# Row 0 of a dilated sliding attention in two halves of 288 tokens, with its loads and row 1's let go in a new order, ahead of a ReLU-squared MLP

## The chip, the cores and the metric

The kernel runs on one core of one Trainium2 chip. The metric is the device time of one execution in microseconds (us). A profile is taken of one execution; its span is about 1.8 us shorter than the time of that execution. TensorE is called PE below, VectorE DVE, ScalarE ACT, GpSimd POOL and SyncE SP, as in the profile.

## The reference, cut to what matters

```python
# q, k, v: (8 rows, 8 heads, 576 tokens, 64); heads 0-3 sliding, 4-7 dilated
scores = scale * np.matmul(q, k.transpose(0, 1, 3, 2))
mask_plain = (rel >= 0) & (rel < 32)
mask_dil   = (rel >= 0) & (rel < 128) & (rel % 4 == 0)
attn = softmax(where(mask, scores, -1e9));  x = attn @ v     # 4608 tokens x 512
h = x @ w_in                                                 # 512 x 2048
out = (np.maximum(h, 0.0) ** 2) @ w_out                      # 2048 x 512
```

A "row" is one of the eight batch rows, 576 tokens; a "chunk" is 512 of the 4608 tokens, one unit of the MLP. Chunk 0 needs nothing but row 0; chunk 1 needs row 1 as well. The first product is `x @ w_in`, the second is with `w_out`.

## The kernel before

The program is in fixed order on each engine. A generator of product matmuls is "pumped": each `pump(n)` puts n small pieces of product work between pieces of attention. A load that must not start too early is let go by a memset into its target on DVE: the load waits for the memset, and the memset for all DVE work in front of it.

```python
load_sliding_qk(0, (nc.sync, nc.scalar))       # row 0, whole
load_dilated_qk(0); load_sliding_v(0); load_dilated_v(0, nc.scalar)
...
transposes_and_scores(0, idle_and_load)        # w_in let go at the third call
...
load_sliding_qk(1); load_dilated_qk(1)         # row 1, right behind row 0
g0 = hidden(0)
pending.append(mm1_part_gen(0, g0, 0, 288))    # chunk 0's first product, tokens 0-287
for a in range(2):
    pump(1); zs.append(av_dilated(0, 1, a))    # row 0's second half beside it
pump(1); x_sliding(0, 1, xs, False)
pump(2); x_dilated(0, 1, zs, False); pump(8)
...; load_w_out(); pump(1000)
pending.append(mm1_part_gen(0, g0, 288, TOKC)) # tokens 288-511
pump(2)
reload_v(1)                                    # row 1's v let go here
pump(1); cast_sliding_qk(1, ...); pump(2)
transposes_and_scores(1, lambda: pump(1)); pump(1000)
pending.append(mm2_by_rows_gen(0, g0)); pump(3)
scores_dilated(1, lambda: pump(3))
...; dk = keep_qk(2)                           # row 2's q, k to scratch
pump(12); cast_v(nc.scalar); attn_values(1, rows_and_load, True)
```

The softmax here doesn't subtract the row's maximum and nothing guards it: scores larger than these inputs give would overflow.

## Time and profile before

| What | Value | Where it is read |
|---|---|---|
| time | 307.47 us, median of 4 (307.22 to 307.62) | runs |
| PE busy | 295.0 us, 96% of the span | busy table of the page |
| row 0's keys landed | 8.26 us | chain in order of time |
| first product starts (half of row 0) | 25.73 us | chain |
| all of row 0 ready | 29.84 us | timeline of ACT |
| v of row 1 let go, landed | 36.2, 54.4 us | timeline of SP, chain |
| chunk 1's first product starts | 64.94 us | chain |

In the chain each line is a start, a length and a piece of work, followed back from the last instruction to what released it. A DMA that stands there means that the program was waiting for it. Behind 64.94 us the two kernels do the same work. The whole difference therefore lies in front of that point. I call that part the opening.

### The profile page before, as it was taken

Reading aid. Unit: us, or ns where it says so; the run is one execution under the profiler, and the core shown is the slowest. Engines: PE = TensorE matmul, PEld = TensorE weight load, DVE = VectorE, ACT = ScalarE, POOL = GpSimd, SP = SyncE. Lnnn points to the kernel's source line nnn. Section 1 sums busy time; section 2 is a strip of 40 time slices with the busy share of each in tenths; the row PEclk is TensorE's granted clock in tenths of the full one; section 3 lists DMA queues with packets and bytes.
Section 4 is the critical chain, followed back from the end, with each engine's and each line's share of the span. In section 5 each row is a group of like instructions: output and inputs, shape, how many; then the busy total and the mean of one; then the engine's idle time right before and its main releaser. Section 6 shows DMA issues by size and latency. Waiting matters only on the chain.

```text
span 307.1 us, 7069 instructions
## 1 busy us (share of the span) xinstructions
PE 295.0 (96%) x2920; PEld 199.0 (65%) x2920; DVE 213.7 (70%) x428; ACT 184.6 (60%) x317; POOL 41.9 (14%) x86
## 2 busy tenths in 40 slices
PE   6789999999899999999999999999999999999995
PEld 2777774444597459745974597459745974684484
DVE  5487682479976697769776977697769775834744
ACT  2586893668933894389438953895389526505610
POOL 4312302006002300230023002300100010000000
PEclk9599999999999999999999999999999999999998
DMA  7999899899979989999859993979520012003004
GB/s 183 249 210 226 142 179 211 186 224 224 276 147 240 266 143 221 226 225 155 178 168 226 152 231 113 228 173 181 142 96 2 0 40 99 2 0 140 0 0 139
DMA packets 83312, 47.91 MB, mean 156 GB/s; under 512 B 67792, under 2 KB 79568, under 8 KB 82896
## 3 DMA queue, kind: packets, MB, share of 16 engines
q1 hardware_dynamic: 75060, 26.12, 41.3%
q0 software_dynamic: 6848, 19.80, 28.3%
q10 hardware_dynamic: 1372, 1.54, 1.8%
q8 instruction: 23, 0.38, 0.5%
q14 instruction: 9, 0.07, 0.1%
HBM read 39.85 MB, written 16.52 MB: 184 GB/s over the span
## 4 chain that ended last, share of the span: by engine, by line
PE 86%; DMA 6%; ACT 3%; SPq 2%; DVE 1%; issue 1%; DVEq 0%; ACTq 0%
PE ph L324 37%; PE pob L374 9%; PE poa L374 9%; PE poe L374 5%; PE poc L374 5%; PE pod L374 5%; DMA sv<-in_v_dram 3%; PE paw L621 3%; PE ph L302 3%; DMA sq<-in_k_dram 2%; SPq L106 2%; PE pav L607 2%; PE py L654 2%; PE ps L556 1%; PE px L636 1%; PE po L345 1%
## 5 line engine op out<-in xcount | busy, mean ns | idle before, releaser
L324 PE MATMUL ph<-xT,wi 128*128 128x512 f16 x512 | 115.8, 379 | 0.0
L290 ACT ACTIVATE rt<-ph 128x512 f16<-128x512 f32 x128 | 75.5, 602 | 32.9 <-PE ph L324 32.6
L324 PEld LDWEIGHTS <-wi 128*128 128x128 f16 x512 | 48.2, 98 | 55.1
L294 DVE TENSOR_TENSOR g<-rt 128x1024 f16<-128x1024 f16 x56 | 38.7, 691 | 35.2 <-ACT rt L290 34.9
L374 PEld LDWEIGHTS <-sm 128*128 128x128 f16 x512 | 47.0, 98 | 4.9
L374 PEld LDWEIGHTS <-g 128*128 128x128 f16 x384 | 35.8, 98 | 6.5 <-DVE g L292 1.1
L374 PE MATMUL pob<-T,sm 128*128 128x256 f16 x256 | 32.5, 272 | 0.0
L374 PE MATMUL poa<-wo,g 128*128 128x256 f16 x256 | 32.1, 273 | 0.0
L660 ACT COPY xT<-py 128x576 f16<-128x576 f16 x16 | 10.2, 638 | 25.8 <-PE py L654 25.7
L394 POOL DMA_DIRECT2D out_dram<-otl x6 | 4.5, 756 | 152.2 <-DVE otl L429 152.2
L590 DVE TENSOR_TENSOR x_d<-paw,rcp_d 72x512 f16<-72x512 f32 x32 | 22.0, 686 | 1.1
L528 ACT ACTIVATE AT<-pz 128x576 f16<-128x576 f32 x32 | 19.0, 653 | 2.3 <-PE pz L575 1.8
L528 ACT ACTIVATE AT<-ps 128x576 f16<-128x576 f32 x32 | 19.2, 659 | 0.7 <-PE ps L538 0.3
L642 ACT COPY xT<-px 128x576 f16<-128x576 f16 x16 | 10.2, 640 | 14.7 <-PE px L636 14.7
L529 DVE TENSOR_TENSOR AT<-AT,maskp 128x576 f16<-128x576 f16 x32 | 14.9, 474 | 4.5 <-ACT AT L528 3.6
L302 PE MATMUL ph<-xT,wi 128*128 128x288 f16 (+1 forms) x128 | 16.6, 272 | 0.9 <-ACT xT L660 0.5
L590 DVE TENSOR_TENSOR x_p<-pav,rcp_p 96x512 f16<-96x512 f32 x24 | 16.5, 687 | 0.8
L529 DVE TENSOR_TENSOR AT<-AT,maskd 128x576 f16<-128x576 f16 x32 | 14.1, 456 | 3.4 <-ACT AT L528 2.3
L374 PE MATMUL pod<-T,g 128*128 128x256 f16 x128 | 16.2, 272 | 0.0
L374 PE MATMUL poc<-T,sm 128*128 128x256 f16 x128 | 16.2, 272 | 0.0
L374 PE MATMUL poe<-wo,sm 128*128 128x256 f16 x128 | 16.1, 273 | 0.0
L145 ACT CAST vd<-sd 128x1024 f16<-128x1024 f32 x16 | 16.1, 1070 | 0.0
(99 smaller groups left out, 369.7 us busy)
## 6 DMA issues: line engine op xcount, KB each, us to landing
sv<-in_v_dram SPq DMA_DIRECT2D x40, 128.0 KB, 4.6
sd<-in_v_dram SPq DMA_DIRECT2D x7, 512.0 KB, 5.9
dk<-in_k_dram POOLq DMA_DIRECT2D x12, 288.0 KB, 6.6
dk<-in_q_dram POOLq DMA_DIRECT2D x12, 288.0 KB, 8.2
out_dram<-otl POOLq DMA_DIRECT2D x6, 512.0 KB, 3.6
out_dram<-otu POOLq DMA_DIRECT2D x6, 512.0 KB, 3.7
wi<-in_moe_w_in_dram POOLq DMA_DIRECT2D x2, 1024.0 KB, 12.1
wo<-in_moe_w_out_dram POOLq DMA_DIRECT2D x4, 512.0 KB, 10.1
```

The costliest lines, as they stand in the source:

```text
L145: nc.scalar.copy(o, i)
L290: nc.scalar.activation(rt[:, o, :], ph[:], ACTF.Relu)
L294: nc.vector.tensor_mul(g[:, ffc - 1 : ffc + 1, :], rt, rt)
L302: nc.tensor.matmul(ph[:, 0 : t1 - t0], wi[:, dmk, ffc * P : ffc * P + P], xs[:, dmk, :], start=(dmk == 0), stop=(dmk == NDM - 1),)
L324: nc.tensor.matmul(ph, wi[:, dmk, ffc * P : ffc * P + P], xs[:, dmk, :], start=(dmk == 0), stop=(dmk == NDM - 1),)
L374: nc.tensor.matmul(acc, lhs[:, k, t * P : (t + 1) * P], rhs[:, k, :], start=(first and k == 0), stop=(k == NK - 1), skip_group_check=True,)
L528: nc.scalar.activation(AT[:, u, 0:UW], ps[:, :, 0 : UW // 2], ACTF.Exp, scale=scale)
L529: nc.vector.tensor_mul(AT[:, u, 0:UW], AT[:, u, 0:UW], mask)
L590: nc.vector.tensor_tensor(out=x[0:w], in0=pv[:, :, :, 0:D], in1=rcp[0:w].unsqueeze(3).to_broadcast([w, 2, HH, D]), op=ALU.mult,)
L621: nc.tensor.matmul(pav[:, e, h * (D + 2) : h * (D + 2) + D + 1], AT[:, 4 + h, off : off + P], vd[:, t, 2 * a + e, h, 0 : D + 1], start=Tru ...
L642: nc.scalar.copy(xT[:, 0:2, t0 : t0 + 288], px[:, 0:UW].rearrange("x (c t) -> x c t", c=2),)
L660: nc.scalar.copy(xT[:, 2:4, t0 : t0 + 288].rearrange("x c (i r) -> x c i r", r=DIL), py[:, 0:UW].rearrange("x (c r i) -> x c i r", c=2, r= ...
```

## The change

Its intent: start row 0's attention as soon as half of its data is there, spread the loads so that each comes when it is needed, give the queues to w_in and w_out in pieces, and run chunk 0's first product in one part with row 1's transposes under it. The core of the diff, cut:

```diff
-    load_sliding_qk(0, (nc.sync, nc.scalar))
+    load_sliding_qk_half(0, 0, nc.sync)
+    load_sliding_qk_half(1, 0, nc.scalar)
...
-        for f0, f1 in ((0, 1024), (1024, 2048)):
+        for f0, f1 in ((0, 512), (512, 1024), (1024, 1536), (1536, 2048)):
...
+    cast_sliding_qk_half(1, 0, nc.scalar)
+    cast_sliding_qk_half(0, 0, nc.vector)
+    nc.vector.memset(sv[:, :, :, 0:1], 0.0)
+    nc.vector.memset(sd[:, :, :, 0:1], 0.0)
+    load_sliding_v(0, 0, 3)
+    load_dilated_v(0, nc.sync, (0,))
+    load_sliding_qk_half(1, 1, nc.sync)        # second half of q, k behind v's first
+    load_sliding_qk_half(0, 1, nc.sync)
+    load_sliding_v(0, 3, 6)
+    load_dilated_v(0, nc.sync, (1,))
... (halves of row 0, interleaved, with idle matmuls between)
+    load_w_out(0, 1)
+    load_dilated_qk(1)
+    load_w_out(1, 4)
...
     g0 = hidden(0)
-    pending.append(mm1_part_gen(0, g0, 0, 288))
...
+    pending.append(mm1_gen(0, g0))             # undivided
+    pump(10)
+    nc.vector.memset(sq[:, :, :, 0:1], 0.0)
+    load_sliding_qk(1)                         # row 1's q, k let go here
+    pump(14)
+    cast_sliding_qk(1, (nc.scalar, nc.vector, nc.scalar, nc.vector))
+    pump(2)
...
-    reload_v(1)
...
     scores_dilated(1, lambda: pump(3))
+    reload_v(1)                                # row 1's v let go here
...
-    pump(12)
+    pump(2)
     cast_v(nc.scalar)
```

More of the change, by code (lines that the diff above doesn't have):

```diff
@@ L73 @@
     wo = wpool.tile([P, NFF, DM], FP16, name="wo")
-    QKTp = const.tile([P, 2, 2, PADP + S], FP16, name="QKTp")
+    QKTp = [const.tile([P, 2, PADP + S], FP16, name=f"QKTp{hp}") for hp in range(2)]
     QKTd = const.tile([P, 2, 2, KPAD + S], FP16, name="QKTd")
@@ L86 @@
     sq = gp.tile([QB, 2, HH, 6 * D], FP32, name="sq", tag="sm")
-    early = tp.tile([QB, 2, 2, 12 * D * 2], FP16, name="early", tag="T")
-    nq_ = early[:, 0].rearrange("p i (j h d) -> p i j h d", j=6, h=HH)
-    nd_ = early[:, 1].rearrange("p i (g x) -> p i g x", g=2)
+    early = tp.tile([QB, 7168], FP16, name="early", tag="T")
+    nq_ = early[:, 0:3072].rearrange("p (i j h d) -> p i j h d", i=2, j=6, h=HH)
+    nd_ = early[:, 3072:6144].rearrange("p (i g x) -> p i g x", i=2, g=2)
+    nqh = early[:, 0:3072].rearrange("p (f i j h d) -> p f i j h d", f=2, i=2, j=3, h=HH)
+    ndh = early[0:72, 3072:7168].rearrange("p (f i g x) -> p f i g x", f=2, i=2, g=2)
     ident = const.tile([P, P], FP16, name="ident")
@@ L100, in load_sliding_qk, with load_sliding_qk_half, load_dilated_qk_half, load_sliding_v @@
             )
-    def load_sliding_v(b):
-        for m in range(NB):
+    def load_sliding_qk_half(i, f, eng):
+        eng.dma_start(
+            out=sq[:, i, :, 192 * f : 192 * (f + 1)],
+            in_=(q, k)[i][0, 0:HH, 288 * f : 288 * (f + 1), :].rearrange(
+                "h (p j) d -> p h (j d)", j=3
+            ),
+        )
+    def load_dilated_qk_half(f):
+        for i, src in ((1, k), (0, q)):
+            s4 = src[0, HH:H, 288 * f : 288 * (f + 1), :].rearrange(
+                "(g e) (p j) d -> e p g (j d)", e=2, j=8
+            )
+            for e in range(2):
+                nc.gpsimd.dma_start(out=ndh[36 * e : 36 * (e + 1), f, i, :, :], in_=s4[e])
+    def load_sliding_v(b, m0=0, m1=NB):
+        for m in range(m0, m1):
             lo = QB * m - PADP
@@ L109, in load_sliding_v, with load_dilated_v @@
             )
-    def load_dilated_v(b, eng):
+    def load_dilated_v(b, eng, ts=(0, 1)):
         vv = v[b, HH:H].rearrange("h (i c) d -> i h (c d)", c=DIL)
-        eng.dma_start(out=sd[PADD:P, 0, :, :], in_=vv[0:QD])
-        eng.dma_start(out=sd[:, 1, :, :], in_=vv[QD - PADD : CL])
+        if 0 in ts:
+            eng.dma_start(out=sd[PADD:P, 0, :, :], in_=vv[0:QD])
+        if 1 in ts:
+            eng.dma_start(out=sd[:, 1, :, :], in_=vv[QD - PADD : CL])
     def load_v(b):
@@ L131, in load_w_in, with load_w_out @@
             )
-    def load_w_out():
-        for j in range(4):
+    def load_w_out(j0, j1):
+        for j in range(j0, j1):
             nc.gpsimd.dma_start(
@@ L157, in cast_sliding_qk, with cast_sliding_qk_half @@
                 )
+    def cast_sliding_qk_half(i, f, eng):
+        copy(
+            eng,
+            nqh[:, f, i],
+            sq[:, i, :, 192 * f : 192 * (f + 1)].rearrange("p h (j d) -> p j h d", d=D),
+        )
     def cast_sliding_v(eng, step, m0=0, m1=NB):
@@ L161, in cast_sliding_v, with cast_dilated_v @@
             copy(eng, vp[:, m : m + step, :, 0:D], sv[:, m : m + step, :, :])
-    def cast_dilated_v(eng, step):
-        for t in range(2):
+    def cast_dilated_v(eng, step, ts=(0, 1)):
+        for t in ts:
             for c in range(0, DIL, step):
@@ L211 @@
     nc.scalar.activation(warm, warm, ACTF.Exp)
-    load_dilated_qk(0)
+    load_dilated_qk_half(0)
     make_identity(nc, ident)
-    load_sliding_v(0)
-    load_dilated_v(0, nc.scalar)
     relf = const.tile([P, QB], FP32, name="relf")
@@ L231 @@
         )
-    nc.vector.memset(QKTp[:, 1, :, 0:PADP], 0.0)
+    for hp in range(2):
+        nc.vector.memset(QKTp[hp][:, 1, 0:PADP], 0.0)
     nc.vector.memset(QKTx[:, 1, 0:PADP], 0.0)
-    nc.vector.memset(QKTd[:, 1, :, 0:KPAD], 0.0)
+    nc.vector.memset(QKTd[:, 1, :, :], 0.0)
     nc.vector.memset(AT[:, :, UW:640], 0.0)
@@ L505, in t_sliding @@
             nc.vector if i else nc.scalar,
-            QKTp[:, i, hp, PADP:].rearrange("x (p j) -> x p j", j=6),
+            QKTp[hp][:, i, PADP:].rearrange("x (p j) -> x p j", j=6),
             p_[:, 0:UW].rearrange("x (j p) -> x p j", j=6),
@@ L525, in t_dilated, with t_sliding_half, t_dilated_half @@
             )
+    def t_sliding_half(hp, f, eng):
+        p_ = pt(f"ph{hp}_{f}", False)
+        for i in (1, 0):
+            for j in range(3):
+                nc.tensor.transpose(
+                    p_[:, 288 * i + QB * j : 288 * i + QB * (j + 1)],
+                    nqh[:, f, i, j, 2 * hp : 2 * hp + 2, :],
+                    ident[0:QB, 0:QB],
+                )
+        t0 = PADP + 288 * f
+        copy(
+            eng,
+            QKTp[hp][:, :, t0 : t0 + 288].rearrange("x i (p j) -> x i p j", j=3),
+            p_[:, 0:UW].rearrange("x (i j p) -> x i p j", i=2, j=3),
+        )
+    def t_dilated_half(i, f, eng):
+        p_ = pt(f"pg{i}_{f}", False)
+        for g in range(2):
+            for n in range(4):
+                o = 288 * (n % 2) + 144 * (n // 2) + 72 * g
+                nc.tensor.transpose(
+                    p_[:, o : o + 72],
+                    ndh[:, f, i, g, P * n : P * (n + 1)],
+                    ident[0:72, 0:72],
+                )
+        for a in range(2):
+            copy(
+                eng,
+                QKTd[:, i, a, KPAD:]
+                .rearrange("x (g n) -> x g n", n=CL)[:, :, QD * f : QD * (f + 1)]
+                .rearrange("x g (p s) -> x g p s", s=2),
+                p_[:, 288 * a : 288 * (a + 1)].rearrange("x (s g p) -> x g p s", s=2, g=HH),
+            )
     def softmax(u, ps, mask):
@@ L529, in softmax, with s_sliding @@
         nc.vector.tensor_mul(AT[:, u, 0:UW], AT[:, u, 0:UW], mask)
-    def s_sliding(b, hp):
-        tiles = [pa(f"ps{b}_{hp}_{half}") for half in range(2)]
-        for half, ps in enumerate(tiles):
+    def s_sliding(b, hp, halves=(0, 1)):
+        tiles = [pa(f"ps{b}_{hp}_{half}") for half in halves]
+        for half, ps in zip(halves, tiles):
             for m3 in range(3):
@@ L539, in s_sliding @@
                         ps[:, e, QB * m3 : QB * (m3 + 1)],
-                        QKTp[r, 1, hp, QB * m : QB * m + P],
-                        QKTp[r, 0, hp, PADP + QB * m : PADP + QB * (m + 1)],
+                        QKTp[hp][r, 1, QB * m : QB * m + P],
+                        QKTp[hp][r, 0, PADP + QB * m : PADP + QB * (m + 1)],
                         start=True,
@@ L544, in s_sliding @@
                     )
-        for half, ps in enumerate(tiles):
+        for half, ps in zip(halves, tiles):
             softmax(2 * hp + half, ps, maskp)
@@ L583, in s_dilated, with s_dilated_half, normalize, av_sliding @@
             softmax(4 + 2 * g + h, ps, maskd)
-    def normalize(b, what, pav, w):
+    def s_dilated_half(t, g):
+        ps = pa(f"pz_{t}_{g}")
+        for h in range(2):
+            for a in range(2):
+                q0 = KPAD + (2 * g + h) * CL + QD * t
+                for e in range(2):
+                    r = slice(D * e, D * (e + 1))
+                    n = 2 * h + a
+                    nc.tensor.matmul(
+                        ps[:, e, QD * n : QD * (n + 1)],
+                        QKTd[r, 1, a, q0 - PADD : q0 - PADD + P],
+                        QKTd[r, 0, a, q0 : q0 + QD],
+                        start=True,
+                        stop=True,
+                    )
+        softmax(4 + 2 * t + g, ps, maskd)
+    def normalize(b, what, pav, w, n=2):
         x = xp.tile([QB, 2, HH, D], FP16, name=f"x{b}_{what}", tag="x")
         rcp = xp.tile([QB, 2, HH], FP32, name=f"rcp{b}_{what}", tag="rcp")
-        pv = pav[0:w, :, 0 : HH * (D + 2)].rearrange("p i (h d) -> p i h d", d=D + 2)
-        nc.vector.reciprocal(rcp[0:w], pv[:, :, :, D])
+        pv = pav[0:w, 0:n, 0 : HH * (D + 2)].rearrange("p i (h d) -> p i h d", d=D + 2)
+        nc.vector.reciprocal(rcp[0:w, 0:n], pv[:, :, :, D])
         nc.vector.tensor_tensor(
-            out=x[0:w],
+            out=x[0:w, 0:n],
             in0=pv[:, :, :, 0:D],
-            in1=rcp[0:w].unsqueeze(3).to_broadcast([w, 2, HH, D]),
+            in1=rcp[0:w, 0:n].unsqueeze(3).to_broadcast([w, n, HH, D]),
             op=ALU.mult,
         )
-        return x
-    def av_sliding(b, mp):
-        pav = pa(f"pav{b}_{mp}")
-        for i in range(2):
-            m = 2 * mp + i
+        return [x[:, i] for i in range(n)]
+    def av_sliding(b, m0, m1):
+        pav = pa(f"pav{b}_{m0}")
+        for i, m in enumerate(range(m0, m1)):
             for h in range(HH):
@@ L613, in av_sliding @@
                 )
-        return normalize(b, f"p{mp}", pav, QB)
+        return normalize(b, f"p{m0}", pav, QB, m1 - m0)
     def av_dilated(b, t, a):
@@ L619, in av_dilated @@
             for h in range(HH):
-                off = e * 288 + a * 144 + t * QD
+                if b == 0:
+                    u, off = 4 + 2 * t + h // 2, e * 288 + (h % 2) * 144 + a * QD
+                else:
+                    u, off = 4 + h, e * 288 + a * 144 + t * QD
                 nc.tensor.matmul(
                     pav[:, e, h * (D + 2) : h * (D + 2) + D + 1],
-                    AT[:, 4 + h, off : off + P],
+                    AT[:, u, off : off + P],
                     vd[:, t, 2 * a + e, h, 0 : D + 1],
@@ L633, in x_sliding @@
             m = 3 * half + m3
-            x = xs[m // 2][:, m % 2].rearrange("p h d -> p (h d)")
+            x = xs[m].rearrange("p h d -> p (h d)")
             for c in range(2):
@@ L650, in x_dilated @@
             for e in range(2):
-                x = xs[a][:, e].rearrange("p h d -> p (h d)")
+                x = xs[2 * a + e].rearrange("p h d -> p (h d)")
                 for c in range(2):
@@ L684, in attn_values @@
         for mp in range(3):
-            xs.append(av_sliding(b, mp))
+            xs += av_sliding(b, 2 * mp, 2 * mp + 2)
             fill()
@@ L688, in attn_values @@
         fill()
-        ys = [av_dilated(b, 0, 0)]
+        ys = av_dilated(b, 0, 0)
         fill()
@@ L692, in attn_values @@
         fill()
-        ys.append(av_dilated(b, 0, 1))
+        ys += av_dilated(b, 0, 1)
         fill()
@@ L696, in attn_values @@
         for a in range(2):
-            zs.append(av_dilated(b, 1, a))
+            zs += av_dilated(b, 1, a)
             fill()
@@ L704 @@
     hold = const.tile([P, 1], FP32, name="hold")
-    cast_sliding_qk(0, (nc.scalar, nc.scalar, nc.vector, nc.gpsimd))
     pj = pmool.tile([P, TOKC], FP32, name="pj", tag="pm")
-    idle_matmuls(pj, 14, TOKC)
-    def idle():
-        idle_matmuls(pj, 5, P)
-    def idle_and_load():
-        idle()
-        n_idle[0] += 1
-        if n_idle[0] == 3:
-            nc.vector.memset(hold, 0.0)
-            nc.gpsimd.memset(hold, 0.0)
-            load_w_in()
-            cast_sliding_v(nc.gpsimd, 2)
@@ L722 @@
-    n_idle = [0]
-    transposes_and_scores(0, idle_and_load)
-    scores_dilated(0, idle)
-    cast_dilated_v(nc.scalar, DIL)
-    xs = [av_sliding(0, 0)]
-    idle()
-    xs.append(av_sliding(0, 1))
-    nc.vector.memset(sq[:, :, :, 0:1], 0.0)
-    nc.vector.memset(nd_[:, :, :, 0:1], 0.0)
-    idle()
-    ys = [av_dilated(0, 0, 0)]
-    idle()
-    x_sliding(0, 0, xs, False)
-    idle()
-    ys.append(av_dilated(0, 0, 1))
-    idle()
-    xs.append(av_sliding(0, 2))
-    idle()
-    x_dilated(0, 0, ys, False)
@@ L742, with idle @@
-    load_sliding_qk(1)
-    load_dilated_qk(1)
-    g0 = hidden(0)
-    pending.append(mm1_part_gen(0, g0, 0, 288))
-    zs = []
-    for a in range(2):
-        pump(1)
-        zs.append(av_dilated(0, 1, a))
-    pump(1)
-    x_sliding(0, 1, xs, False)
-    pump(2)
-    x_dilated(0, 1, zs, False)
-    pump(8)
+    idle_matmuls(pj, 12, TOKC)
+    def idle(n=3):
+        idle_matmuls(pj, n, P)
+    cast_sliding_qk_half(1, 0, nc.scalar)
+    cast_sliding_qk_half(0, 0, nc.vector)
+    nc.vector.memset(sv[:, :, :, 0:1], 0.0)
@@ L757 @@
+    nc.vector.memset(sd[:, :, :, 0:1], 0.0)
[5 more added lines that the diff above has]
+    load_dilated_v(0, nc.sync, (1,))
+    t_sliding_half(0, 0, nc.scalar)
+    t_sliding_half(1, 0, nc.vector)
     nc.vector.memset(hold, 0.0)
     nc.gpsimd.memset(hold, 0.0)
-    load_w_out()
+    load_dilated_qk_half(1)
+    t_dilated_half(1, 0, nc.scalar)
+    idle()
+    s_sliding(0, 0, (0,))
@@ new lines @@
+    t_dilated_half(0, 0, nc.vector)
+    s_sliding(0, 1, (0,))
+    cast_sliding_v(nc.gpsimd, 3, 0, 3)
+    cast_dilated_v(nc.gpsimd, DIL, (0,))
+    load_w_in()
+    idle(4)
+    s_dilated_half(0, 0)
+    s_dilated_half(0, 1)
+    cast_sliding_qk_half(1, 1, nc.scalar)
+    cast_sliding_qk_half(0, 1, nc.scalar)
+    idle(9)
+    xs = av_sliding(0, 0, 2)
+    xs += av_sliding(0, 2, 3)
+    idle(4)
+    ys = av_dilated(0, 0, 0)
+    idle(2)
+    t_sliding_half(0, 1, nc.scalar)
+    t_sliding_half(1, 1, nc.scalar)
@@ new lines @@
+    x_sliding(0, 0, xs, False)
+    ys += av_dilated(0, 0, 1)
+    s_sliding(0, 0, (1,))
+    t_dilated_half(1, 1, nc.scalar)
+    s_sliding(0, 1, (1,))
+    t_dilated_half(0, 1, nc.vector)
+    x_dilated(0, 0, ys, False)
+    idle()
+    s_dilated_half(1, 0)
+    s_dilated_half(1, 1)
+    cast_sliding_v(nc.gpsimd, 3, 3, 6)
+    cast_dilated_v(nc.gpsimd, DIL, (1,))
+    load_w_out(0, 1)
+    load_dilated_qk(1)
+    load_w_out(1, 4)
+    idle(6)
+    xs += av_sliding(0, 3, 5)
+    xs += av_sliding(0, 5, 6)
@@ new lines @@
+    idle(4)
+    zs = av_dilated(0, 1, 0)
+    idle(4)
+    zs += av_dilated(0, 1, 1)
+    idle(4)
+    x_sliding(0, 1, xs, False)
+    idle(4)
+    x_dilated(0, 1, zs, False)
+    idle(4)
+    g0 = hidden(0)
+    pending.append(mm1_gen(0, g0))
[5 more added lines that the diff above has]
+    pump(2)
+    for hp in range(2):
+        for i in (1, 0):
+            t_sliding(1, hp, i)
+            pump(1)
@@ L760 @@
     pump(1000)
-    pending.append(mm1_part_gen(0, g0, 288, TOKC))
-    pump(2)
     def reload_v(b):
@@ L768, in reload_v @@
         load_v(b)
+    pending.append(mm2_by_rows_gen(0, g0))
+    for g in range(2):
+        s_sliding(1, g)
+        pump(2)
+        for i in (1, 0):
+            t_dilated(1, g, i, True)
+            pump(2)
+    scores_dilated(1, lambda: pump(3))
     reload_v(1)
-    pump(1)
-    cast_sliding_qk(1, (nc.scalar, nc.vector, nc.scalar, nc.vector))
+    nc.gpsimd.tensor_copy(hold, wo[:, NFF - 1, DM - 1 :])
+    nc.gpsimd.tensor_copy(hold, sd[:, 1, HH - 1, DIL * D - 1 :])
+    dk = keep_qk(2)
     pump(2)
-    transposes_and_scores(1, lambda: pump(1))
-    pump(1000)
-    pending.append(mm2_by_rows_gen(0, g0))
-    pump(3)
-    scores_dilated(1, lambda: pump(3))
-    nc.vector.memset(hold, 0.0)
-    nc.gpsimd.memset(hold, 0.0)
-    dk = keep_qk(2)
-    pump(12)
     cast_v(nc.scalar)
@@ L812 @@
                 pump(2)
+            pump(2)
         else:
```

## The prediction

> **What bounds the kernel now.** I read the page's slices first, then its chain by share, then the chain in order of time, because the change touches only the first rows. The busy tenths say that TensorE (PE) is full from the fourth slice (23 us) to the end:
>
> ```profile
> PE   6789999999899999999999999999999999999995
> PEclk9599999999999999999999999999999999999998
> DMA  7999899899979989999859993979520012003004
> ```
>
> So the time is the start-up, plus the PE work, plus PE's gaps. The change can gain only before the point at which chunk 1's first product starts, because everything behind that is the same work. In the chain in order of time (start, length, what) that point is 64.94:
>
> ```profile
> 0.75 7.51 DMA sq<-in_k_dram
> 8.28 0.96 DVE early L147
> 9.29 0.66 PE pt L499 x6
> ...
> 25.04 0.65 ACT xT L660
> 25.73 0.40 PE ph L302 x2
> ...
> 29.13 6.17 PE ph L302 x52
> ...
> 44.00 10.41 DMA sv<-in_v_dram
> 54.56 1.48 ACT vp L145
> 56.08 0.41 PE pav L607 x8
> ...
> 64.94 7.36 PE ph L324 x34
> ```
>
> Three things stand there. Row 0's queries and keys arrive at 8.3 us. The first product starts at 25.7, on half of row 0. And row 1's values land at 54.4, just as PE runs out of other work: the timeline by engine shows how small the gap is, and when the values were asked for.
>
> ```profile
> 36.18 10.99 SPq L106 DMA_DIRECT2D sv<-in_v_dram  x6
> ...
> 48.61 0.43 PE L575 MATMUL pz<-QKTd 64*128 64x72 f16 x16
> ...
> 50.59 0.06 DVE L779 MEMSET hold<- 128x1 f32 x1
> ...
> 56.08 0.41 PE L607 MATMUL pav<-vp,AT 128*128 128x65 f16 x8 [0.45 <-ACT vp L145]
> ```
>
> The loads began at 36.2, took 18 us beside w_out, and cost PE 0.45 us. From 28.1 to 64.8 the table by stretches gives DMA shares of 0.84 to 1.27 except in 33.6 to 36.2 (0.42): the queues are nearly always busy here, so when a load is let go decides what it competes with.
>
> **What the Trainium skill says.** "DMA: Bandwidth & Descriptors", section "Queues, rings and completion order": each DMA engine goes round-robin between the queues that have work for it, a packet at a time. The trace agrees: row 1's q and k, 0.59 MB each, were issued at 22.94 and 23.37 beside w_in and landed 6.9 and 11.3 us later. Same page, "Issuing engines are not separate DMA queues": moving loads between issuing engines gives no bandwidth, so taking row 0's dilated values from ACT to SP gains nothing by itself. "TensorE: Matmul & The Clock Gate", section "Architectural detail", says that ACT and DVE are strict FIFO: a memset that lets a load go waits for all earlier DVE work. The same page's "What's actually happening" gives half clock after an idle window of about 3.4 us; here PE idled 2.94 us before 9.29 (somewhat less than that window), and the table by stretches shows a clock of 0.50 from 10 to 15 us.
>
> **The change part by part.**
>
> *Undivided first product.* 52 matmuls of 288 columns took 6.17 us (119 ns each) and 8 of 224 took 0.85 to the next start (106 ns): 64 x 119 + 64 x 106 = 14.4 us. 34 of 512 columns took 7.36 us (216 ns): 64 x 216 = 13.8 us. Saved: 0.6 us of PE. But the product cannot start until both halves of row 0 are transposed.
>
> *Row 0 in halves, start T0 of the first product.* First-half q, k are 0.59 MB sliding plus 0.29 MB dilated. Summing the page's GB/s slices (1.875 us each) gives 0.37 MB by 3.75 us and 0.91 by 5.6, so they land near 5.5 instead of 8.3. But DVE's set-up, which ended at 5.4, grows by about 0.5 us (memset of all 1280 columns of the dilated keys; 512 columns took 0.27), so its cast ends near 6.95 and the transposes start at 7, 2.3 us earlier. That cast also lets the v loads go, so the queues run nearly empty for about 2 us (issue to first bytes took that long at the start: 7 GB/s in the first slice). Then v's first half (0.65 MB), dilated half 1 (0.29) and sliding half 1 (0.59) follow: 1.5 MB at 250 GB/s from 8.5 gives 14.7 us for the second q. From there its chain is: cast 0.83, transposes 0.5, two evictions on ACT 1.3, scores 0.3, four exps 2.4 interleaved with evictions 0.7 and 0.8, last mask 0.5, four normalizations 3.2 on DVE (0.9 each, the narrow one 0.5), transposes 0.4, xT copies 1.3: about 12.5 us, so 27.2. The second v half (0.92 MB, mostly 256-byte rows) starts near 15 together with w_in (2.1 MB): 3.0 MB at 210 GB/s end at 29.5, the last dilated values perhaps at 25 to 27, then 1.2 us of GpSimd cast (0.61 per 512 columns), two AV groups and a copy, 3 us: 29 to 31. I take T0 = 28 (before: all of row 0 was ready at 29.85, but 27 of the divided matmuls were done by then).
>
> *PE work behind T0.* Before, 29.85 to 64.8 is 35.0 us. Taking out 1.3 of gaps, 11.2 of first product (37 x 0.119 + 64 x 0.106) and 13.8 of second leaves 8.6 for row 1. After: T0 + 13.8 + 13.8 + 8.6 = T0 + 36.2, without gaps. At T0 = 28 that would be 64.2: a gain of 0.6 us.
>
> *Gap for row 1's q, k.* They are let go after 10 pumps (20 matmuls), and 16 pumps = 32 matmuls = 6.9 us later PE needs their casts. DVE reaches the memset some 0.6 us late, so PE gives them 6.3 us. Alone they need about 7 us as at the start (7.51), beside w_out 11.7 as in the trace; plus a cast of 0.95. Gap 1.6 to 6.3; I take 3.
>
> *Gap for row 1's v.* This is the largest term. The load moves from 36 us, early in row 1's work, to behind the last dilated scores. Those stand at T0 + 13.8 + 1.1 (transposes) + 15 pumps of second product 6.5 + score and transpose groups 1.9 = T0 + 23.3, plus the gap above. From them the trace takes 1.98 us to the next DVE memset (48.61 to 50.59); the six sliding issues of row 2 took 3.25 us with a landing of 3.2 to 4.6 us for each, so the last lands about 6.9 after the first issue; the cast takes 1.48. Sum 10.4 us. PE has 0.4 + 5 pumps = 2.5 us of work meanwhile, then waits 7.9 us. Before, it waited 0.45.
>
> *Tail.* From the first AV to chunk 1: 56.08 to 64.8, 8.7 us, unchanged. End of the stage = 28 + 23.3 + 3 + 10.4 + 8.7 = 73.4 against 64.8: +8.6 us. Row 2's scratch copy is held until v has landed, so it comes near 71 and its transposes follow some 13 us later; the two extra pumps there (0.86 us) just cover it. Sum: 307.5 + 8.6 = 316.
>
> **The rivals.** (a) *Row 0 comes in so early that it pays.* Break-even needs T0 plus the q, k gap near 22.4. For: the chain starts 2.3 us earlier, and halves overlap DMA with work. Against: from 15 to 25 us ACT (4.13 and 3.17 of each 5) and DVE (4.13 and 4.63) were already mostly busy, and that work isn't removed; DVE alone has some 14 us of it after 6. With T0 = 24 and a gap of 1.6 the sum is 3.2 us over break-even: 310.7; only a smaller v gap as well makes it 305 or less. (b) *The queues decide, not the issue order*: w_out is out of the way when v is asked for, so v lands quickly, and before it landed at 54.4 anyhow. This is true of the queue, but v is asked for at about 56 in my sum, so it costs time still; it makes 312 if T0 is 26 and the first gap 1. (c) *Clock.* PE waiting 7.9 us falls to half clock and up to 2 us of the tail are added, and v's second half comes late behind w_in (T0 = 31): 320 or more.
>
> **Range and chances.** The v gap follows from program order and I hold it nearly certain; T0 (24 to 31) and the q, k gap (1.6 to 6.3) are estimates worth several us each way. A kernel tuned this finely, with counts of idle matmuls fitted, speaks for a result not much worse, so I shade 316 to 315, with 304.5 to 321. Over 2% slower (313.7) needs T0 plus gap above 28.6: 0.56. Within 2%: 0.36. Faster by 2% needs T0 near 16 and no gap for q and k, or a slip in my reading: 0.08.
>
> **What would show it.** Step by step in the profile after: sliding q, k landing near 5.5 and the first transposes at 7; the first 512-column product near 28; a PE idle of 2 to 6 us in that product before row 1's sliding transposes, ended by casts from q or k; the v issues 2 us behind the last dilated scores of row 1, and a PE idle of 7 to 8 us ended by the cast of v; chunk 1's first product near 73. It is wrong if that product starts at 65 or sooner, or if the v loads are issued before the scores are done.

## The result, and the profile after

The changed kernel took 327.07 us (median of 4, 325.92 to 327.50) against 307.47. The ratio is 1.063, with a 95% interval of 1.060 to 1.066: slower. Ratios here are the mean time of one kernel's runs over that of the other's from the same rounds, so they are not quite the ratio of the medians quoted.

The 40 slices of the page after (8.1 us each), the same three rows as were shown of before:

```profile
PE   7589919919998999999999999999999999999995
PEclk9757987977999999999999999999999999999999
DMA  5999960087999999999896999489930003003003
```

PE has a 1 in its sixth and in its ninth slice, where before it was full from the fourth on. The clock is at 5 to 7 in several slices, and the DMA row has a 6 and two zeros in slices six to eight: the queues stand still from about 47 to 65 us, in the middle of the stretch in which they had been busy before.

The chain in order of time of the kernel after:

```profile
0.74 4.95 DMA sq<-in_k_dram
...
29.57 4.06 PE ph L352 x18
...
34.65 11.66 DMA sq<-in_k_dram
...
47.27 0.66 PE pt L527 x6
...
67.14 3.44 DMA sv<-in_v_dram
...
72.35 0.60 PE pav L687 x8
...
82.86 8.20 PE ph L352 x38
```

The first half's keys land at 5.7 us, 2.6 us sooner than the whole did. The first product nevertheless starts only at 29.57. Then the chain runs through two loads of row 1: its keys, let go at 34.65 and landed at 46.3, and its values, the last of which lands at 70.6. Chunk 1 starts at 82.86 in place of 64.94: 17.9 us later. The medians differ by 19.6 us: the profiled execution of the kernel before took 308.89 us, 1.4 us above its median, and in a later trace of the same opening (of the run with v late alone, below) what follows row 0's first transposes comes about 1.2 us sooner.

The two waits on PE's timeline, in brackets with what ended them:

```profile
47.27 0.66 PE L527 MATMUL pt<-ident,early 96*128 96x96 f16 x6 [6.75 <-ACT early L166]
...
72.35 0.60 PE L687 MATMUL pav<-vp,AT 128*128 128x65 f16 x8 [7.15 <-ACT vp L166]
```

The table by stretches of the same trace shows what PE did meanwhile (stretch; length; busy us and instruction count of PE, PE weight loads, DVE, ACT, POOL; clock; DMA share; GB/s):

```profile
40.00:47.30 7.30, 0.55 (x4) 0.06 (x3) 1.66 (x3) 1.21 (x3) 0.00 (x0) 0.89 0.86 196
47.30:53.60 6.30, 6.30 (x40) 3.44 (x42) 3.06 (x5) 3.62 (x6) 0.19 (x1) 0.58 0.01 4
53.60:65.20 11.60, 11.60 (x121) 5.81 (x121) 5.85 (x16) 6.66 (x13) 0.00 (x0) 1.00 0.01 1
65.20:72.35 7.15, 0.00 (x1) 0.00 (x0) 0.00 (x0) 1.47 (x1) 0.00 (x0) 0.81 0.88 201
72.35:82.80 10.45, 10.45 (x109) 5.86 (x109) 7.32 (x18) 6.05 (x9) 2.20 (x5) 0.80 0.65 133
```

PE is idle in the first and fourth stretch (6.75 us waiting for the casts of row 1's q and k, 7.15 us for the cast of v). In the stretch after each, the clock is 0.58 and 0.80. And from 47.3 to 65.2 the DMA share is 0.01: nothing was on the queues, and the load that PE would wait for next had not been asked for.

### The profile page after: what moved, and what is told of

Same layout as the page of the kernel before. It is cut to its first block, busy times and chain, and to the rows that moved or that the text cites. A ratio compares the mean times of both kernels' runs of the same rounds, so it can differ in the third digit from the quotient of the medians. Undisturbed runs are those within 1.5% of the kernel's fastest.

```text
span 325.1 us, 6864 instructions
## 1 busy us (share of the span) xinstructions
PE 298.6 (92%) x2823; PEld 194.7 (60%) x2823; DVE 213.2 (66%) x422; ACT 183.9 (57%) x301; POOL 48.9 (15%) x92
## 3 DMA queue, kind: packets, MB, share of 16 engines
q0 software_dynamic: 8352, 19.80, 27.2%
## 4 chain that ended last, share of the span: by engine, by line
PE 84%; DMA 8%; ACT 4%; DVE 1%; SPq 1%; issue 1%; ACTq 0%; DVEq 0%
PE ph L352 37%; PE pob L402 9%; PE poa L402 9%; DMA sq<-in_k_dram 5%; PE poe L402 4%; PE poc L402 4%; PE po L373 4%; PE pod L402 4%; PE paw L704 3%; DMA sq<-in_q_dram 2%; PE pav L687 2%; PE pz L639 2%; ACT AT L592 1%; PE px L719 1%; PE ps L620 1%; PE py L737 1%
## 5 line engine op out<-in xcount | busy, mean ns | idle before, releaser
L352 PE MATMUL ph<-xT,wi 128*128 128x512 f16 x576 | 132.4, 383 | 0.1
L318 ACT ACTIVATE rt<-ph 128x512 f16<-128x512 f32 x144 | 85.0, 601 | 36.4 <-PE ph L352 36.1
L352 PEld LDWEIGHTS <-wi 128*128 128x128 f16 x576 | 54.6, 98 | 62.0 <-issue 0.9
L322 DVE TENSOR_TENSOR g<-rt 128x1024 f16<-128x1024 f16 x63 | 43.5, 691 | 46.4 <-ACT rt L318 46.1
L687 PE MATMUL pav<-vp,AT 128*128 128x65 f16 x192 | 11.1, 206 | 8.7 <-ACT vp L166 8.3
L373 PE MATMUL po<-wo,g 128*128 128x512 f16 x64 | 18.3, 402 | 0.0
L670 DVE RECIPROCAL rcp_d<-paw 72x8 f32<-72x8 f32 x32 | 6.4, 199 | 18.0 <-PE paw L704 18.0
L671 DVE TENSOR_TENSOR x_p<-pav,rcp_p 96x512 f16<-96x512 f32 (+1 forms) x25 | 16.6, 665 | 0.9
L687 PEld LDWEIGHTS <-AT 128*128 128x128 f16 x192 | 10.2, 106 | 10.9 <-issue 10.2
```

What stands on the lines that cost most here:

```text
L318: nc.scalar.activation(rt[:, o, :], ph[:], ACTF.Relu)
L322: nc.vector.tensor_mul(g[:, ffc - 1 : ffc + 1, :], rt, rt)
L352: nc.tensor.matmul(ph, wi[:, dmk, ffc * P : ffc * P + P], xs[:, dmk, :], start=(dmk == 0), stop=(dmk == NDM - 1),)
L373: nc.tensor.matmul(po, g[:, ffc, t * P : (t + 1) * P], wo[:, ffc, :], start=(ffc == 0), stop=(ffc == NFF - 1),)
L671: nc.vector.tensor_tensor(out=x[0:w, 0:n], in0=pv[:, :, :, 0:D], in1=rcp[0:w, 0:n].unsqueeze(3).to_broadcast([w, n, HH, D]), op=ALU.mult,)
L687: nc.tensor.matmul(pav[:, i, h * (D + 2) : h * (D + 2) + D + 1], AT[:, u, off : off + P], vp[:, m, h, 0 : D + 1], start=True, stop=True,)
```

## The experiments

Theory: the time is lost because row 1's loads are let go too late and in the wrong company, which makes two waits, each with a stretch of half clock behind it. Rivals: the queues are the limit whatever the order; or row 0 in halves, or the undivided product, costs the time by itself.

### One load let go early, the other left

```diff
     load_sliding_qk(1)
+    reload_v(1)
...
-    reload_v(1)          # was behind scores_dilated(1)
```

> The changed kernel with one thing moved: row 1's value loads are let go right behind row 1's query and key loads (about 34.8 us) in place of behind row 1's last dilated scores (64.5 us). Theory (the order in which the loads are let go costs the time): the 7.15 us wait of TensorE for the cast of v goes, and with it the half clock that follows it (about 1.8 us of the 10.5 us tail, which took 8.7 before): 327 to about 318 us; the 6.75 us wait for row 1's keys stays. Rival (the queues are the limit, whatever the order): v now shares with w_out and with q and k, the wait for the keys grows by as much as the other shrinks, and the time stays at 324 us or more.

Measured: 318.86 us (317.98 to 319.39), ratio 1.036. The wait for v fell to 0.25 us and the tail (from the first value product to chunk 1) to 9.3 us; the wait for the keys stayed at 6.32 us. The rival is out: SP issued v beside the keys, from 35.65 to 48.48 us, and the keys landed no later relative to their issue (11.23 us).

```diff
     x_dilated(0, 0, ys, False)
+    nc.vector.memset(sq[:, :, :, 0:1], 0.0)
+    load_sliding_qk(1)
...
-    pump(10)
-    nc.vector.memset(sq[:, :, :, 0:1], 0.0)
-    load_sliding_qk(1)
-    pump(14)
+    pump(24)
```

> The changed kernel with row 1's query and key loads let go once row 0's second half is cast and transposed (about 22 us) in place of 10 pumps into chunk 0's first product (34.2 us); the value loads stay late. Theory: they land by about 36 us, the 6.75 us wait before row 1's transposes goes and with it about 2.6 us of half clock behind it: 327 to about 318 us. Rival (queues are the limit): the loads take bandwidth from w_in, chunk 0's first product waits for its later pieces instead, and the time stays at 324 us or more.

Measured: 319.92 us (318.90 to 320.98), ratio 1.039. The 6.75 us wait became two of 0.54 and 0.57 us. The wait for v stayed at 7.03 us. The gain of 7.2 us is 2 us short of the expectation; the two waits that are left make 1.1 of them. The first product did not wait for w_in, so the rival is out too.

### Both early: the repaired kernel

The edit is both of the above, with v let go at 10 pumps into the product.

> Both moves: row 1's queries and keys let go at about 22 us, its values 10 pumps into chunk 0's first product (about 34 us). Theory: both waits and both half-clock stretches go, 18 us in all: about 308 to 309 us, level with the kernel before, because row 0 in halves starts the product at 29.6 us with 36.2 us of work behind it against the 64.9 us of before. If row 0 in halves cost something of its own that I have not seen, 312 us or more; if it gains, 305 or less.

Measured: 310.60 us (309.82 to 311.44), ratio 1.009 (1.005 to 1.013). So 16.5 of the 19.6 us come from where two calls stand in the program. Some 3 us were left, and the expectation of "level" missed. The chain of this run shows where to look:

```profile
8.94 7.24 DMA sq<-in_q_dram
...
29.29 10.10 PE ph L352 x46
```

Row 0's second half of queries is let go at 8.94, lands at 16.18, and everything up to the product at 29.29 hangs on it.

### Why the keys took so long: w_out held back

```diff
-    load_w_out(1, 4)
...
     cast_sliding_qk(1, (nc.scalar, nc.vector, nc.scalar, nc.vector))
+    nc.gpsimd.tensor_copy(hold[0:QB, :], sq[:, 1, HH - 1, 6 * D - 1 :])
+    load_w_out(1, 4)
```

> The changed kernel with the last three quarters of w_out held until row 1's keys have landed; row 1's loads where the change has them (34.2 us). Tells why those keys take 11.7 us from issue to landing. Theory (sharing with w_out): alone they take about 7 us and land near 41.7 in place of 46.3, so the wait shrinks from 6.75 to about 2 us, too short for half clock: 327 to about 320 us. Rival (the loads are simply let go too late, and take as long alone): 325 to 327 us.

Measured: 318.94 us (318.54 to 320.20), ratio 1.037. The chain of this run has the load of the keys:

```profile
33.82 6.67 DMA sq<-in_k_dram
```

The load took 6.67 us in place of 11.66, PE waited 1.75 us, and from the first transposes to the first scores it took 3.8 us in place of 6.3. So this load was slow because it shared with w_out. That the time came out 1 us below the expectation is not the theory's merit: in this trace the first product began at 28.20 in place of 29.57. PE waited nowhere for the later w_out.

### The late v alone, in the kernel before

```diff
-    reload_v(1)          # early in row 1's work
...
     scores_dilated(1, lambda: pump(3))
+    reload_v(1)
```

> The kernel before with one part of the change alone: row 1's value loads let go behind the last dilated scores of row 1 (about 50.6 us) in place of early (36.2 us). Theory: the cast of v then ends near 61 to 62 us in place of 56.0, and TensorE, which runs out of work at 54.4 to 55.6, waits some 6 us and comes out at half clock: 307.5 to about 314 us. Rival (the queues decide when v lands, w_out is ahead of it anyway): within 1.5 us of 307.5.

Measured: 317.92 us (316.71 to 318.28), ratio 1.033: slower, as the theory said, and by 4 us more than expected. The timeline of PE in this run has the wait in brackets:

```profile
63.02 0.60 PE L607 MATMUL pav<-vp,AT 128*128 128x65 f16 x8 [8.71 <-ACT vp L145]
```

SP took 6.42 us to issue the six loads, against 3.04 in the changed kernel. In this kernel row 2's scratch copies are let go at the same point and share the queues (issued from 49.7 us, between the loads of v); the changed kernel holds them until v has landed. I had not counted that. That they are what made v slower here is argued from this order; no run separates it.

### The half clock behind the waits

The edit puts idle matmuls on zeros ahead of a wait (28 of 512 columns ahead of both, then 26 ahead of one at a time).

```diff
+    idle_matmuls(pa("fill0")[:, 0, :], 28, TOKC)   # ahead of row 1's transposes
...
+    idle_matmuls(pa("fill1")[:, 0, :], 28, TOKC)   # ahead of attn_values(1, ...)
```

> The changed kernel with 28 idle matmuls of 512 columns (6 us at full clock) put on TensorE ahead of each of the two long waits, for row 1's keys and for row 1's values; loads as in the changed kernel. The waits themselves stay, but TensorE is not idle in them. Theory: the clock granted behind them stays at full speed, worth about 2.6 us behind the first and 1.8 us behind the second: 327 to about 322.5 us. Rival (the half clock is hidden, or another engine sets the pace there): 326 to 327 us.

Measured: 326.68 us, but in two groups (324.01, 324.70, 328.65, 328.81), ratio 1.061 (1.053 to 1.069). The profiled run, of the lower group, had a clock of 1.00 in all five stretches of the table above. What made the upper group slow is open; the time decides nothing. So I filled one wait at a time.

> The changed kernel with 26 idle matmuls of 512 columns (5.6 us) ahead of the wait for row 1's keys alone. Theory: the stretch from the first transposes of row 1 to its first scores takes 3.8 us in place of 6.3, and the time falls from 327.1 to about 324.7 us. Rival (the half clock is hidden, or the work on zeros slows something else): 326.5 us or more.

Measured: 323.65 us (323.11 to 324.84), ratio 1.054. From the first transposes to the first scores it took 3.8 us in place of 6.3. That is 2.4 us; the rest of the 3.4 us is not the clock's. In this trace the keys were let go at 34.01 in place of 34.65, ahead of the edit.

> The changed kernel with 26 idle matmuls of 512 columns ahead of the wait for row 1's values alone. Theory: the tail from the first value product to chunk 1's first product takes 9.1 us in place of 10.5, and the time falls from 327.1 to about 325.7 us. Rival: 326.5 us or more.

Measured: 325.58 us (324.56 to 326.76), ratio 1.060. The tail took 9.9 us in place of 10.5, with a wait of 0.94 us for ACT in it; with both waits filled it took 9.3. The half clock is real and on the path: in the traces 2.4 us behind the first wait and 0.6 to 1.2 behind the second.

### The undivided product, in the kernel before

```diff
-    pending.append(mm1_part_gen(0, g0, 0, 288))
...
     x_dilated(0, 1, zs, False)
+    pending.append(mm1_gen(0, g0))
```

with idle matmuls in place of the pumps in front of it.

> The kernel before with one part of the change alone: chunk 0's first product undivided, starting when all of row 0 is transposed, with idle matmuls where its first part had run beside row 0's last groups. Loads keep their order. Theory: 27 of the 64 divided groups' matmuls (3.2 us) had run before all of row 0 was ready, and undividing saves 0.6 us of TensorE: 307.5 to about 310 us. Rival (undividing is free because PE has slack elsewhere): within 0.8 us of the kernel before.

Measured: 307.41 us (306.67 to 307.99), ratio 1.000 (0.998 to 1.002). My theory fell. The timeline of PE shows why:

```profile
27.19 7.93 PE L324 MATMUL ph<-xT,wi 128*128 128x512 f16 x36 [0.29 <-ACT xT L660]
```

Without the product in between, the whole of row 0 is ready at 27.1 us, not at 29.84. But not all of this is the edit's doing. The last copy of row 0 on ACT's timeline, in the kernel before, in the run with v late (whose opening is that of the kernel before) and in this run:

```profile
29.21 0.63 ACT L660 COPY xT<-py 128x576 f16<-128x576 f16 x1
27.98 0.63 ACT L660 COPY xT<-py 128x576 f16<-128x576 f16 x1
26.50 0.64 ACT L660 COPY xT<-py 128x576 f16<-128x576 f16 x1 [0.45 <-PE py L654]
```

The same opening ended 1.2 us apart in two executions; from 10 to 15 us their clock was 0.50 and 0.66. Against the second of these traces, the divided product delays row 0 by 1.5 us. That is less than the 3.2 us of its work that was done by then, and yet the times are level; the rest I did not trace. Beside this, row 0 in halves, with its product at 29.29 in the repaired kernel, is 2.1 us slower than row 0 whole. In five traces with the changed kernel's opening as it stands, all of row 0 is ready between 28.9 and 30.0 us (29.2 in the repaired kernel), so the loss is 1.8 to 2.9 us against this one trace of row 0 whole.

### What row 0 in halves lacks

Edits of the repaired kernel. First, the product divided again:

```diff
     x_dilated(0, 0, ys, False)
+    pending.append(mm1_part_gen(0, g0, 0, 288))
...
-    idle(6)
+    pump(2)
     xs += av_sliding(0, 3, 5)
... (each later idle(4) in row 0 becomes pump(1); tokens 288-511 follow as in the kernel before)
```

> The repaired kernel (both of row 1's loads early, 310.6 us) with chunk 0's first product divided again at 288 tokens, its first part put in place of the idle matmuls beside row 0's second half. Theory: row 0 in halves made all of row 0 ready no more than 0.6 us sooner, and the undivided product gave up about 3 us of product work that the kernel before had done by then; some 6 of the 16 groups of 4 (0.48 us each, 2.9 us) now run beside row 0's second half: 310.6 to about 307.5 us. Rival (ACT and DVE set the pace there, and relu and square delay row 0's chain by as much): 310 to 311 us.

Measured: 309.84 us (309.58 to 310.50), ratio 1.007. Most of the expected 3 us did not come: as I read the timelines, DVE and PE took up the product's work in row 0's chain, and 0.80 us went to a wait for w_in at 34.95.

Then, with the product undivided, the second half's q and k loaded at once:

```diff
     load_sliding_qk_half(0, 0, nc.sync)
     load_sliding_qk_half(1, 0, nc.scalar)
+    load_sliding_qk_half(0, 1, nc.sync)
+    load_sliding_qk_half(1, 1, nc.scalar)
...
-    load_sliding_qk_half(1, 1, nc.sync)
-    load_sliding_qk_half(0, 1, nc.sync)
```

> The repaired kernel (310.6 us) with row 0's second half of sliding queries and keys loaded at once, behind the first half and ahead of v, in place of behind v's first half. Theory: the second half's chain starts when its queries land (16.4 us), while the queues were nearly empty from 6 to 8 us; loaded at once they land by about 9 us, and the product starts 2 us sooner: 308.5 us. Rival (the second half is held by ACT, DVE and TensorE at half clock, or v's first half now comes that much later): 310 us or more.

Measured: 310.02 us (309.69 to 310.59), ratio 1.008. The second half was cast by 15.3 us, but PE took it up at 16.59, behind the first half's value products in program order, and the first half's dilated keys came later (PE waited 1.95 us for them). The rival holds in part: other loads came later for it.

Then both of these edits together:

> The repaired kernel (310.6 us) with both further moves: chunk 0's first product divided again, and row 0's second half of sliding queries and keys loaded at once. Each alone gave about 0.7 us (309.8, 310.0). Theory (they act in different places, the product's overlap and the load's arrival): they add, about 309 us. Rival (both run into the same bound, row 0's chain on ACT, DVE and a half-clock TensorE): 309.5 to 310 us.

Measured: 307.86 us (307.47 to 308.56), ratio 1.002 (1.000 to 1.004). Together they gave more (0.7% by the ratios) than each alone (0.16% and 0.13%, which is within the repaired kernel's interval of 1.005 to 1.013). Why, no run shows.

Then, with neither, more idle matmuls in row 0:

```diff
-    idle(4)              # behind load_w_in()
+    idle(16)
...
-    idle(9)
+    idle(14)
     xs = av_sliding(0, 0, 2)
     xs += av_sliding(0, 2, 3)
-    idle(4)
+    idle(16)
     ys = av_dilated(0, 0, 0)
-    idle(2)
+    idle(26)
```

> The repaired kernel (310.6 us) with more idle matmuls of 128 columns between row 0's groups: 16 in place of 4, 14 of 9, 16 of 4 and 26 of 2. Nothing else moves. In the repaired kernel the granted clock was 0.70 from 8 to 16 us, 0.50 from 16 to 24 and 0.61 from 24 to 29.5, where the kernel before had 0.96 to 1.00 from 15 us on. Theory (the half clock stretches row 0's chain of small groups, about 0.2 us each on ten groups): the clock rises and the product starts 1 to 2 us sooner: 309 us. Rival (ACT, DVE or the loads set the pace there): 310.5 us or a little more.

Measured: 311.29 us (310.31 to 312.65), ratio 1.013 (1.011 to 1.016), not faster. The table by stretches of this run:

```profile
8.00:16.00 8.00, 6.50 (x125) 5.61 (x121) 5.00 (x12) 3.26 (x6) 6.45 (x10) 1.00 1.04 207
16.00:24.00 8.00, 4.74 (x94) 4.04 (x94) 3.32 (x9) 5.98 (x11) 5.48 (x9) 0.86 1.23 231
```

The clock rose from 0.70 and 0.50 to 1.00 and 0.86, and the product started no sooner (28.75 on PE's timeline, against 28.63). So the half clock from 8 to 24 us is off the path, as far as this run shows, unlike behind the two waits. From 24 to 29.5 us the clock stayed at 0.58 (0.61 in the repaired kernel), so that stretch is not tested.

Last, the divided product and the early second half, with the sliding part of that half cast and transposed ahead of the first half's dilated part (and idle matmuls of 14, 12 and 10 between groups):

```diff
     load_dilated_qk_half(1)
+    cast_sliding_qk_half(1, 1, nc.scalar)
+    cast_sliding_qk_half(0, 1, nc.vector)
+    idle(14)
+    t_sliding_half(0, 1, nc.scalar)
+    t_sliding_half(1, 1, nc.vector)
     t_dilated_half(1, 0, nc.scalar)
... (the same four calls are taken out where they stood)
```

> An attempt to beat both: row 1's loads early, product divided, row 0's second half loaded at once and its sliding part cast and transposed while the dilated loads and v still arrive, and more idle matmuls in row 0. If the second half's chain was held by its place in program order (in the run with early loads TensorE took it up at 16.6 us though the data were there by 13.8), it starts near 10 us and the result is 306 to 307.5 us, level with or below the kernel before; if the bound is ACT and DVE work, 308.5 to 309.5 us.

Measured: 307.88 us (306.26 to 308.81), ratio 1.001 (0.999 to 1.004). Level with the kernel before, within noise. No version that I ran beats it clearly.

## Why the prediction was right or wrong

The direction and both waits were forecast; the size was not. It said 315 us, with 304.5 to 321 to hold it, and +7.5 us came out as +19.6. The opening's own sum said 73.4 us and the profile shows 82.86. Two of its steps failed: the gap for row 1's q and k was taken at 3 us and was 6.75, and the half clock behind the waits was left out of the sum. By its steps:

| Step as the prediction put it | Predicted | Measured | Difference |
|---|---|---|---|
| start of the first product, T0 | 28 | 29.57 | +1.6 |
| from T0 to the last dilated scores, without gaps and half clock | 23.3 | 23.8 | +0.5 |
| gap for row 1's q and k | 3 (1.6 to 6.3) | 6.75 | +3.75 |
| half clock behind that gap | not in the sum | 2.4 | +2.4 |
| last dilated scores to the first value product | 10.4 | 9.84 | -0.6 |
| tail | 8.7, "unchanged" | 10.5 | +1.8 |

The differences add up to 9.45 us; 82.86 less 73.4 is 9.46. (23.8 is 62.51, the last dilated scores on PE, less 29.57, 6.75 and 2.4; 2.4 is the 6.27 us from the first transposes to the first scores, less the 3.83 that the run with w_out held took for it.)

**The gap for q and k was mis-sized.** The mechanism was right: the run with them early removed the wait, and the one with w_out held cut it to 1.75 us. Both ends of the range were in the prediction, 7 us alone and 11.7 beside w_out. I took a middle value, and the gap came out above the upper end. But the order of issue decides which end holds: the change puts w_out on the queue in front of them, issued from 23 to 32 us, and that load lasted until 47. The measured landing was 11.66 us. The 11.7 was misread besides: in the trace of before these loads ran from 22.94 to 34.67 us, beside w_in and row 1's dilated loads; w_out was let go only at 33.6. That the 11.66 us beside w_out agree with it is luck. Where two sizes belong to two cases, the case is to be decided; a mean belongs to neither.

**The clock was a rival, and should have been a term.** The prediction named the half clock after a wait of 7.9 us, gave it up to 2 us, and left it out of the sum. The trace of before had already shown it, at 10 to 15 us. It also came behind the q and k wait, which I had not considered. The filled runs put it at 2.4 us there and at 0.6 to 1.2 behind the wait for v. The tail was mis-sized by another 0.43 us: the change leaves 24 product matmuls for it where there had been 22. These terms and the 3.75 above account for most of the miss.

**The gap for v was right** in cause, place and size: 7.15 us against 7.9. The step argued from program order alone, that a memset on DVE stands behind the masks of the last scores. The run with v early and the run of the kernel before with v late show it from both sides. Rival (b), that w_out would be out of the way by then, held: the last load of v landed soon after its issue, and it was still too late.

**T0 was 1.6 us late, and that turns the small gain into a loss.** Row 0's chain from the landing of the second q was put at 12.5 us, and the repaired kernel took 13.1; its landing was put at 14.7 and was 16.4 in the changed kernel. The other path, by the last dilated values, did not bind: put at 25 to 27, they were cast from 22.0. The prediction's T0 + 36.2 gives 64.2 with T0 = 28, "a gain of 0.6 us", and 65.8 with 29.57, a loss of 1 us; the repaired kernel, with no long wait, began chunk 1 at 66.62. Against row 0 whole and the product undivided (27.2) halves lose about 2 us. Why they lose is shown in part: the second q waited on the queue behind v, and its place in program order held it too; moving both, with the product divided (in the last run), made up for it. And the queues were nearly empty from 6 to 8 us, with a share of 0.16 and 0.36, as predicted.

**The shade towards the kernel before was wrong.** The counts of idle matmuls had looked like signs of a fitted kernel, and that moved the number from 316 to 315. It was no evidence about this change.

**What the skill was cited for.** That queues take turns fits the run with w_out held (6.67 us in place of 11.66), though no run shows turns packet by packet. That the issuing engine gives no bandwidth, no run separates. That DVE works in order shows where the memset for v, at 64.50, starts as the last masks end (63.53 to 64.53).

**Does the sum close?** It does when the changed kernel is set against the repaired one, which differs from it only in where the two loads stand: 82.86 less 66.62 is 16.24 us. The waits make 12.54 of it (6.75 and 7.15, less 0.54, 0.57 and 0.25). The clock behind the first wait makes 2.2 (6.27 us from the first transposes to the first scores against 4.07, without the wait of 0.57 in it), the tail 1.24 (10.51 against 9.27), and the start of the product 0.28. The other 1.7 us of the 17.9 lie between the repaired kernel and the kernel before, whose trace is itself a late one.

What stays open: why executions of the same opening lie 1 us apart, what makes the upper group of the run with both waits filled slow, and the part of the loss by halves that is not the second q's.

## What to carry to other kernels

A load that is let go by an instruction on an in-order engine starts no sooner than all work ahead of that instruction, so when it is moved, add landing and cast to its new place and compare with the work that the waiting engine still has. A late load isn't paid by the wait alone: what is ahead of it on the shared queues stretches it, and PE came out of the waits of about 7 us at half clock here, but not out of one of 1.75 us. When work is interleaved with a chain, the time at which the chain ends says nothing of how long it takes alone; run it alone before comparing another order with it. And a trace is one execution: compare its time with the median before reading a difference of 1 us from it.

## What the Trainium skill lacked or had wrong

- "DMA: Bandwidth & Descriptors", section "Queues, rings and completion order", gives the round-robin between queues but no figure for what a load loses by it. Here row 1's keys, 0.59 MB with as much of queries just ahead, took 11.66 us beside w_out and 6.67 us without it.
- "TensorE: Matmul & The Clock Gate", section "What's actually happening", gives half clock after an idle window of about 3.4 us. In the changed kernel the clock fell to 0.50 by 12 to 13 us though no idle of PE from 7 us on had lasted over 0.9 us by then; PE was only partly busy. The page tells of another kernel whose short idles between groups made the clock swing ("A second HAM failure mode: psum-queue depth-cycling"), but has no threshold for that; its "Part 4: PE-mode transpose" says that transposes count as busy in another way, which no run here separates.
- That page's "What's actually happening" puts the ramp at under 1% of a typical span. It speaks of the ramp at a kernel's start. Here two further stretches of half clock, behind waits, cost 2.4 and up to 1.2 us in the traces, 1.1% of 327 us together, so a sum for such a kernel needs a term for each long wait.
